# Float32 transposes that accumulate the tap sums of the first batch, and a shorter conversion of float64 weights

## The chip, the core and the metric

The kernel runs on one core of a Trainium2 chip. The metric is device time in microseconds (us) from launch to the last instruction; smaller is better. The engines are called TensorE (PE in the profile), VectorE (DVE), ScalarE (ACT), GpSimd (POOL) and SyncE (SP). Each runs its own instructions in program order and waits on semaphores for the others.

## What is computed

The reference is a windowed mix over time with softmax weights, then a two-stage mixer. Shapes: x is 8 x 4096 x 192 (batch, time, channel), the weights of the mix are 8 x 4096 x 8 heads x 7 taps, the four mixer matrices arrive as float64.

```python
w = softmax(weight_gen, axis=-1)                       # 7 taps per head
out[b,s,h,g] = sum_k w[b,s,h,k] * x_pad[b, s+k, h, g]  # 6 zeros in front of each batch
xt = out.transpose(0, 2, 1)
h  = relu(xt @ w_tok1) @ w_tok2                        # mixes over time, 4096 -> 256 -> 4096
u  = out + h.transpose(0, 2, 1)
h2 = relu(u @ w_ch1) @ w_ch2                           # mixes over channels, 192 -> 1536 -> 192
result = u + h2
```

## The kernel before, in words

A batch is cut into 8 chunks of 512 time steps (CT = 4 steps in each of 128 partitions); with 8 batches there are 64 chunks. The program has two parts.

**The first batch** (lines 876 to 962) has no mixer work to run beside. For each chunk m it does the following.

- VectorE multiplies x by the softmax weights for all 7 taps, in two instructions (`products`, line 327, tiles called prk: four taps, then three). The seventh product is added to the fifth by an accumulating DMA that GpSimd issues (line 330).
- TensorE adds the remaining six products into PSUM by multiplying each with an identity matrix (`sums`, line 341, tile tapsum, 12 matmuls of 384 columns per chunk; the trace shows a float32 matmul as two passes). ScalarE copies the sum to SBUF (line 346, tile xa: the attention output of the chunk).
- Between the first four taps and the other two, TensorE does work of the chunk before: the first token matmul, 8 instructions (`token1_first`, line 517, tile th), and the turn of xa to channel-major form by 8 matmuls against the identity (`turn_first`, line 353, tile turn). ScalarE copies the turned chunk out (line 360) into xb (chunks 0 and 1) or into ts, which ScalarE's DMA queue spills to DRAM (lines 363 and 364). Chunks 6 and 7 are not turned here: in the main part VectorE turns them (line 291) and SP stores them (line 297).
- Meanwhile float64 weights are converted to float32 with integer steps on their two 32-bit halves (`convert`, lines 144 to 160). ScalarE makes a mask in three steps (lines 154 to 156), VectorE combines shifted bits in three (lines 158 to 160). One conversion of 1024 columns per chunk turns out the token weights w1 of that chunk; conversions of 768 columns for the channel weights are put between (w1 halves for chunks 1 and 3, c2 for chunk 5 and after), and the token weights w2 follow. raw tiles hold the float64 input; three of them take turns, so a load waits until VectorE has finished the conversion three loads before.
- The softmax of the next two chunks (lines 178 to 187) runs in odd chunks; its exponential (line 180) is on ScalarE, between a subtraction (179) and a sum (181) on VectorE.

The order of instructions here is the order of the code, with `run` taking turns between lists of steps.

At the end of the batch come the last token matmul, h1 = relu of the result in two parts (lines 474 and 476), and `token2(0)` (line 534), which also needs the first converted and split w2 weights (cast on ScalarE and difference on VectorE, lines 165 and 166).

**The main part** (from line 963) goes over the 64 chunks. For each: twelve column blocks of `channel1` (line 599, tiles ph) in six pairs, relu in two parts by ScalarE and VectorE (605, 606, tile h), `channel2` (line 617, into acc), the turn of the result (671, 672) and its store. `token1` and `token2` of later chunks, the attention of the next batch (`attention`, lines 210, 224 and 228) and the remaining conversions are put between them by a planner, `pump`, which works with estimated costs and times. ScalarE and VectorE split the weights of the last channel matrix on lines 459 to 461 (tile w2s).

Of the kernel before, what the change touches and what calls it, by code (L numbers as in the profile page):

```python
# [12 lines left out]
F32 = mybir.dt.float32  # L13
F32R = mybir.dt.float32r
U32 = mybir.dt.uint32
AF = mybir.ActivationFunctionType
# [5 lines left out]
def mixer_kernel(ctx: ExitStack, tc: tile.TileContext, x, wg, wt1, wt2, wc1, wc2, out):  # L22
    nc = tc.nc
# [20 lines left out]
    SM = 2  # L44
    XA = 4
    PR = 5
    FT = NCH - 2
    TAPS = [(0,), (1, 2), (3, 4), (5, 6)]
    Q = 32

# [4 lines left out]
    ctx.enter_context(tc.manual_schedule())  # L55
    pro = None

    below = const.tile([P, 1], F32, name="below")
    nc.gpsimd.memset(below, -float(np.nextafter(np.float32(2.0 ** -15), np.float32(0))))

# [50 lines left out]


    NV = 1024
    LOW30 = float(np.array(0x3FFFFFFF, np.uint32).view(np.float32))

    staged = {"raw": 0, "val": 0}
    raw_tag, tag_of = {}, {}
# [1 line left out]
    def raw_tile(tag=None):  # L121

        n = staged["raw"]
        staged["raw"] += 1
        if pro is not None and n % 3 == 0:
            return pro.tile([P, NV, 2], U32, tag="raw", name="raw")
        if tag is None:
            tag = "w1" if (n - n // 3 - 1) % 2 else "raw"
        raw_tag[n] = tag
        return p1.tile([P, NV, 2], U32, tag=tag, name="raw")  # L130

    def val_tile():

# [10 lines left out]
    def convert(raw, n, out):  # L144

        yield "gate", 0, lambda: state["vals"] < 2
        state["vals"] += 1
        yield "w", 0, lambda: free["val"]
        v = val_tile()[:, 0:n]
        out.append(v)  # L150
        bits = v.bitcast(U32)
        low, high = raw[:, 0:n, 0], raw[:, 0:n, 1]
        act, stt = nc.scalar.activation, nc.vector.scalar_tensor_tensor
# [4 lines left out]
        yield "v", cost, lambda: stt(bits, high, 3, bits, op0=ALU.logical_shift_left, op1=ALU.bitwise_and)  # L158
        yield "v", cost, lambda: stt(bits, low, 29, bits, op0=ALU.logical_shift_right, op1=ALU.bitwise_or)
        yield "v", cost, lambda: stt(bits, high, 0xC0000000, bits, op0=ALU.bitwise_and, op1=ALU.bitwise_or)  # L160

    def split(hi, lo, v):

# [157 lines left out]
    def products(m, pro):  # L321
        src, (wn, j) = xt.pop(m), wnt.pop(m)
        prs = []
        for k0, k1 in ((0, KA), (KA, K)):
            pr = pro.tile([P, KA, CT, D], F32, tag="pr", name="prk", bufs=3)[:, 0:k1 - k0]
            x_k, w = taps(src, wn, j, k0, k1)
            nc.vector.tensor_mul(pr.rearrange("p k t (h g) -> p k (t h) g", h=H), x_k, w)
# [6 lines left out]
    def sums(m, prs, between):  # L334
        acc = new_xa(m)
        ps = ps_pro.tile([P, 2, 512], F32, tag="sum", name="tapsum", bufs=2)
        half = CT // 2
        for k0, k1 in ((0, KA), (KA, len(prs))):
            for n in range(2):
                for k in range(k0, k1):  # L340
                    nc.tensor.matmul(ps[:, n, 0:half * D], ident, prs[k][:, n * half:(n + 1) * half, :],  # L341
                                     start=k == 0, stop=k == len(prs) - 1)
            if k0 == 0:
                between()
        for n in range(2):
            nc.scalar.copy(acc[:, n * half:(n + 1) * half, :], ps[:, n, 0:half * D])

    def turn_first(m):

        ps = ps_pro.tile([P, 2, 512], F32, tag="turn", name="turn")  # L350
        for n, d in enumerate((0, D - P)):
            for c in range(CT):
                nc.tensor.matmul(ps[:, n, c * P:(c + 1) * P], xat[m][:, c, d:d + P], ident, start=True, stop=True)  # L353
# [4 lines left out]
        for n, c0 in ((0, 0), (1, DC)):  # L358
            to = t[c0:P, n, :].rearrange("p (n b c) -> p c n b" if m == 0 else "p (n c b) -> p c n b", c=CT, b=Q)
            nc.scalar.copy(to, ps[c0:P, n, :].rearrange("p (c n b) -> p c n b", c=CT, b=Q))  # L360
# [469 lines left out]
    def prefetch(m):  # L830

        if m % SM == 0:
            load_wg(m)
        load_x(m)
# [41 lines left out]
    with tc.tile_pool(name="pro", bufs=1) as pro, \  # L876
            tc.tile_pool(name="ps_pro", bufs=1, space=bass.MemoryType.PSUM) as ps_pro:
        ident = pro.tile([P, P], F32, name="ident")
        make_identity(nc, ident)
        warm = pro.tile([P, 1], F32, name="warm")  # L880
        nc.scalar.activation(warm, ident[:, 0:1], AF.Exp)
        prefetch(0)
        th = ps_pro.tile([P, 2, 512], F32, tag="th", name="th")

        def token1_first(m, v):
            token1_float(th, v.rearrange("p (c r) -> p c r", c=CT), m,
                         0 if m == 0 else None, CT - 1 if m == NCH - 1 else None)

        def start(items):

            items = iter(items)
            for _ in range(5):
                next(items)[2]()
            return items

        between = {1: ("w1", 0), 3: ("w1", 1), 5: ("c2", 0)}
        w1_v, w1_it = {}, {}

        def start_w1(m):
            fetch_w1(m)  # L900
            w1_v[m] = []
            w1_it[m] = start(convert(rawt.pop(("w1", m)), CT * R, w1_v[m]))

        def others():

            if m > 0:
                token1_first(m - 1, v_old)
                turn_first(m - 1)

        run(softmax(0))  # L910
        start_w1(0)
        prefetch(1)
        start_w1(1)
        behind, channel = (), None
        for m in range(NCH):
            prs = products(m, pro)
            if m + AHEAD < NCH:
                prefetch(m + AHEAD)
            run(w1_it.pop(m), softmax(m + 1) if (m + 1) % SM == 0 and m + 1 < NCH else ())
            v, = w1_v.pop(m)  # L920
            if m == NCH - 1:
                fetch_channel("w1", 2)
                run(w2_it, until="n")
                fetch_w2(1)
                run(w2_it)
                token1_first(m - 1, v_old)
                sums(m, prs, lambda: None)
            if m == NCH - 2:
                load_wg(NCH)
            current, channel = channel, None  # L930
            if m in between:
                fetch_channel(*between[m])
                channel = start(convert_channel(*between[m], pro))
            if m + 2 < NCH:
                start_w1(m + 2)
            elif m + 2 == NCH:
                fetch_w2(0)
            nc.sync.dma_start(s0[m], v)
            run(behind)
            behind = ()  # L940
            if m == NCH - 2:
                sums(m, prs, others)
# [4 lines left out]
            if m < NCH - 2:  # L947
                sums(m, prs, others)
# [12 lines left out]
        pro = None  # L961
        state["vals"] = 1
# [198 lines left out]
```

## Time and profile before

| | us |
|---|---|
| median of 3 runs | 2110.72 (2109.53 to 2110.96) |
| profiled execution, first to last instruction | 2109.3 |
| TensorE busy | 2071.5 (98%) |
| VectorE busy | 1539.7 (73%) |
| ScalarE busy | 1444.6 (68%) |
| GpSimd busy | 165.1 (8%) |
| first matmul of token2(0), the end of the first batch | 118.30 |

The trace holds no time before the first and after the last instruction; the span of 2109.3 lies 1.4 us under the median of the runs. Busy shares are averages over the whole program, and the two parts have different limits. So the profile is read here by stretches: busy time per engine in a window, and timelines, where each row has the start, the length, the engine and line, what it writes and reads, how many instructions are merged, and in brackets how long the engine was idle before it and what released it.

### The profile page before, as it was taken

How to read it: one execution, taken by the hardware profiler on the slowest of the kernel's cores; microseconds unless marked ns; L12 is line 12 of the kernel's file. 1: busy time of each engine (PE TensorE's matmuls, PEld its weight loads, DVE VectorE, ACT ScalarE, POOL GpSimd, SP SyncE). 2: the span in 40 equal slices, each digit the busy share in tenths (PEclk: the TensorE clock that was granted, in tenths of full speed). 3: DMA queues.
4: the chain of work that ended last, by engine and by line, in shares of the span. 5: the costliest groups of instructions: out<-in, count | busy, mean ns of one | idle time of the engine just before them, and what ended most of it. 6: DMA issues, size and time to landing. Idle time of an engine off the chain costs nothing.

```text
span 2109.3 us, 32111 instructions
## 1 busy us (share of the span) xinstructions
PE 2071.5 (98%) x12736; PEld 1684.9 (80%) x12736; DVE 1539.7 (73%) x1760; ACT 1444.6 (68%) x2226; POOL 165.1 (8%) x202
## 2 busy tenths in 40 slices
PE   6989999999999999999999999999999999999998
PEld 4767888788887888888888888888888888888887
DVE  8979988888888777777777787777777765343433
ACT  5578776677776676667667667666766766676665
POOL 1001111000101000000000010000100000000000
PEclk9999999999999999999999999999999999999999
DMA  9965767777876776666666676666666555321221
GB/s 298 270 222 170 202 179 226 239 199 210 239 217 179 205 202 170 189 158 180 173 198 175 191 185 163 174 184 199 177 184 192 149 169 138 90 71 51 57 63 23
DMA packets 167350, 366.97 MB, mean 174 GB/s; under 512 B 16680, under 2 KB 106024, under 8 KB 151840
## 3 DMA queue, kind: packets, MB, share of 16 engines
q1 hardware_dynamic: 139808, 285.74, 42.6%
q0 software_dynamic: 26496, 77.61, 18.9%
q8 instruction: 100, 1.64, 0.3%
q10 hardware_dynamic: 896, 1.57, 0.2%
q14 instruction: 50, 0.41, 0.1%
HBM read 225.13 MB, written 70.52 MB: 140 GB/s over the span
## 4 chain that ended last, share of the span: by engine, by line
PE 93%; DVE 4%; DMA 1%; ACT 1%; issue 0%; SPq 0%; POOL 0%; ACTq 0%; DVEq 0%; POOLq 0%
PE acc L617 40%; PE ph L599 35%; PE up L534 7%; PE th L497 4%; PE tapsum L341 3%; PE th L517 2%; PE th L499 2%; DVE h L606 1%; DVE pr L210 1%; PE turn L353 1%; PE acc L634 0%; DMA xt<-in_x_dram 0%; DMA prk<-prk 0%; DMA out_dram<-out_tile 0%; DVE pr L224 0%
## 5 line engine op out<-in xcount | busy, mean ns | idle before, releaser
L617 PE MATMUL acc<-h,w2s 128*128 128x512 f32 x3800 | 886.8, 391 | 4.1 <-DVE w2s L460 4.1
L617 PEld LDWEIGHTS acc<-h,w2s 128*128 128x128 f32 x3800 | 710.8, 188 | 151.0 <-DVE w2s L460 4.5
L605 ACT ACTIVATE h<-ph 128x1024 fp32r<-128x1024 f32 x384 | 394.5, 1027 | 345.6 <-PE ph L599 298.1
L606 DVE SCALAR_TENSOR_TENSOR h<-ph,h 128x1024 fp32r<-128x1024 f32 x384 | 468.2, 1220 | 117.4 <-ACT h L605 116.6
L599 PE MATMUL ph<-u_hi,w_hi 64*128 64x512 f32 x2304 | 337.9, 394 | 5.3 <-DVE h L606 3.7
L599 PE MATMUL ph<-u_lo,w_hi 64*128 64x512 f32 x2304 | 329.3, 388 | 0.5 <-ACT u_lo L574 0.3
L599 PE MATMUL ph<-u_hi,w_lo 64*128 64x512 f32 x2304 | 328.1, 387 | 0.0
L210 DVE TENSOR_TENSOR pr<-xt,wg 128x768 f32<-128x768 f32 x336 | 311.3, 947 | 0.3
L599 PEld LDWEIGHTS ph<-u_hi,w_hi 64*128 64x128 f32 x2304 | 213.7, 184 | 72.5 <-issue 19.4
L599 PEld LDWEIGHTS ph<-u_lo,w_hi 64*128 64x128 f32 x2304 | 219.0, 184 | 47.3 <-ACT u_lo L574 0.7
L599 PEld LDWEIGHTS ph<-u_hi,w_lo 64*128 64x128 f32 x2304 | 218.4, 184 | 46.7
L228 POOL DMA_DIRECT2D xa<-pr x168 | 144.7, 861 | 1392.4 <-DVE pr L224 846.9
L681 ACT COPY out_tile<-oa 32x256 f32<-32x256 f32 x504 | 203.5, 404 | 8.0
L546 DVE TENSOR_TENSOR uf<-up,uf 64x512 f32<-64x512 f32 x63 | 43.0, 683 | 213.6 <-ACT uf L542 213.6
L534 PE MATMUL up<-w,h 128*128 128x512 f32 x630 | 161.0, 401 | 2.1 <-ACT up L528 2.1
L224 DVE TENSOR_TENSOR pr<-pr 128x768 f32<-128x768 f32 x168 | 160.1, 953 | 3.4
L534 PEld LDWEIGHTS up<-w,h 128*128 128x128 f32 x630 | 114.2, 188 | 43.4 <-issue 13.4
L528 ACT COPY up<-xb 128x1024 f32<-128x1024 f32 x63 | 64.1, 1017 | 75.5 <-DVE h L606 70.2
L269 DVE TENSOR_TENSOR xh<-xa,xh 128x768 fp32r<-128x768 f32 x48 | 45.8, 954 | 91.4 <-ACT xh L266 91.3
L497 PE MATMUL th<-xh,w 128*128 128x384 f32 x384 | 112.5, 358 | 0.0
L681 ACT COPY out_tile<-oc 32x256 f32<-32x256 f32 x252 | 101.6, 403 | 6.9 <-DVE oc L674 2.4
L499 PE MATMUL th<-xh,w 128*128 128x192 f32 x384 | 96.2, 250 | 0.0
(89 smaller groups left out, 1709.3 us busy)
## 6 DMA issues: line engine op xcount, KB each, us to landing
w<-s SPq DMA_DIRECT2D x96, 1024.0 KB, 5.5
xa<-pr POOLq DMA_DIRECT2D x168, 384.0 KB, 5.1
xt<-in_x_dram SPq DMA_DIRECT2D x56, 960.0 KB, 7.6
out_dram<-out_tile SPq DMA_DIRECT2D x128, 192.0 KB, 4.0
xs<-t SPq DMA_DIRECT2D x58, 384.0 KB, 4.6
xb<-xs SPq DMA_DIRECT2D x348, 64.0 KB, 5.2
raw<-in_moe_w_tok_dram SPq DMA_DIRECT2D x16, 1024.0 KB, 6.0
s<-w POOLq DMA_DIRECT2D x8, 1024.0 KB, 7.0
```

Source lines behind the costliest of these rows:

```text
L210: nc.vector.tensor_mul(t.rearrange("p t (h g) -> p (t h) g", h=H).rearrange("p (o n) g -> p o n g", o=1), x_k, w)
L224: nc.vector.tensor_add(sums[m], sums[m], prt.pop(m))
L228: nc.gpsimd.dma_start(xat[m].rearrange("p t d -> p (t d)"), sums[m].rearrange("p t d -> p (t d)"), accum_op=ALU.add)
L497: nc.tensor.matmul(th[:, r, 0:2 * D], w[:, c, 0, rs], xh[:, c, :], start=i + c == 0, stop=False, skip_group_check=True)
L499: nc.tensor.matmul(th[:, r, 0:D], w[:, c, 1, rs], xh[:, c, 0:D], start=False, stop=c == CT - 1, skip_group_check=True)
L528: nc.scalar.copy(up.rearrange("p k (n b c) -> p (k n) c b", c=CT, b=Q), xb.rearrange("p k (n c b) -> p (k n) c b", c=CT, b=Q))
L534: nc.tensor.matmul(up[:, n, :], h1[:, k, d], w[:, l, k * N:(k + 1) * N], start=k == 0 and j == 0 and not seeded, stop=k == KR - 1 and j == ...
L599: nc.tensor.matmul(ph[:, j, :], w[rows, k, p * P:(p + 1) * P], u[rows, k], start=n == 0, stop=n == len(steps) - 1)
L605: nc.scalar.activation(h[:, :, 0, :], ph, AF.Relu)
L606: nc.vector.scalar_tensor_tensor(h[:, :, 1, :], ph, 0.0, h[:, :, 0, :].bitcast(F32), op0=ALU.max, op1=ALU.subtract)
L617: nc.tensor.matmul(acc[:, n, :], w2s[:, f, d], h[:, j, l, :], start=False, stop=f == NF - 1 and i == len(steps) - 1, skip_group_check=True)
L681: nc.scalar.copy(dst, src[to:to + Q].rearrange("p (n e d) -> p n e d", n=2, d=Q)[:, n])
```

## The change

Two things are changed, both in the first batch and in every conversion.

1. *Tap sums.* All seven products are summed on TensorE, by transposes in transpose mode: the product is the stationary operand, the identity the moving one, and PSUM accumulates the seven results (42 transposes of 128 x 128 per chunk). The DMA that added the seventh product is gone. The sum comes out turned, so the turn of `turn_first` is gone too: ScalarE copies the six 128-column blocks out once as they are (line 363, tile sum) and once as the turned chunk (line 375, five copies). Six further transposes (`turn_back`) turn the sum back to xa, in the middle of the next chunk's sums; `token1_first` of the chunk before follows after them. All eight chunks are turned and spilled here (FT = NCH), so VectorE's two turns in the main part are gone. The sums of a chunk are now issued ahead of the conversion steps of chunk m + 2 on ScalarE; the loads of these weights (`fetch_w1`) stay where they were.

2. *Conversion.* ScalarE makes two values: from the low half a number with the top three bits of it (tile few), and from the high half a float scaled by 2 to the power -112 (tile val). VectorE shifts val left by 3 and joins few (line 170), then joins the sign bit (line 171). That is two steps on each engine for three. The tile few takes a buffer that other tiles use at other times: half of a w2 tile or a pr tile in the first batch, the xh tile in the main part (one buffer).

The core of the diff:

```diff
-    FT = NCH - 2
+    FT = NCH
...
-        yield "s", 950, lambda: act(v, high.bitcast(F32), AF.Abs)
-        yield "s", 1050, lambda: act(v, v, AF.Sign, bias=below[:, 0:1])
-        yield "s", 950, lambda: act(v, v, AF.Relu, scale=LOW30)
+        yield "s", 950, lambda: act(few, low, AF.Copy, scale=THREE[0], bias=THREE[1])
+        yield "s", 950, lambda: act(v, high.bitcast(F32), AF.Copy, scale=2.0 ** -112)
         cost = 70 + n * 1.05
-        yield "v", cost, lambda: stt(bits, high, 3, bits, op0=ALU.logical_shift_left, op1=ALU.bitwise_and)
-        yield "v", cost, lambda: stt(bits, low, 29, bits, op0=ALU.logical_shift_right, op1=ALU.bitwise_or)
-        yield "v", cost, lambda: stt(bits, high, 0xC0000000, bits, op0=ALU.bitwise_and, op1=ALU.bitwise_or)
+        yield "v", cost, lambda: stt(bits, bits, 3, few, op0=ALU.logical_shift_left, op1=ALU.bitwise_or)
+        yield "v", cost, lambda: stt(bits, high, 0x80000000, bits, op0=ALU.bitwise_and, op1=ALU.bitwise_or)
...
-        last = prs.pop()
-        nc.gpsimd.dma_start(prs[KA].rearrange("p t d -> p (t d)"), last.rearrange("p t d -> p (t d)"),
-                            accum_op=ALU.add)
...
+    def transpose(out, data, start):
+
+        nc.tensor.matmul(out, data, ident, is_transpose=True, start=start, stop=True, skip_group_check=True)
+
+    NB = CT * D // P
+
+    def sums(m, prs, between=(), after=()):
+
+        ps = ps_pro.tile([P, 2, 512], F32, tag="sum", name="tapsum", bufs=2).rearrange("p k n -> p (k n)")
+        for k, pr in enumerate(prs):
+            if k == KA:
+                for do in between:
+                    do()
+            flat = pr.rearrange("p t d -> p (t d)")
+            for j in range(NB):
+                transpose(ps[:, j * P:(j + 1) * P], flat[:, j * P:(j + 1) * P], k == 0 and j % 4 == 0)
+        for do in after:
+            do()
+        sumt[m] = p1.tile([P, CT, D], F32, tag="pr", name="sum", bufs=PR).rearrange("p t d -> p (t d)")
+        nc.scalar.copy(sumt[m], ps[:, 0:NB * P])
...
+        for c in range(2):
+            for n, rows, j, of in ((0, slice(0, P), 0, slice(0, P)), (1, hi, 1, lo)) if c == 0 else \
+                    ((0, lo, 1, hi), (0, hi, 2, lo), (1, hi, 2, hi)):
+                nc.scalar.copy(to[n][rows, c], blocks[of, j])
...
+    def turn_back(m):
+
+        t = sumt.pop(m)
+        ps = ps_pro.tile([P, 2, 512], F32, tag="turn", name="turn").rearrange("p k n -> p (k n)")
+        for j in range(NB):
+            transpose(ps[:, j * P:(j + 1) * P], t[:, j * P:(j + 1) * P], j % 4 == 0)
+        nc.scalar.copy(new_xa(m).rearrange("p c d -> p (c d)"), ps[:, 0:NB * P])
...
             if m + 2 < NCH:
-                start_w1(m + 2)
+                fetch_w1(m + 2)
...
             run(behind)
             behind = ()
+            if m > 0:
+                sums(m, prs, (lambda: turn_back(m - 1),), (lambda: token1_first(m - 1, v_old),))
+            else:
+                sums(m, prs)
+            if m in between:
+                channel = start(convert_channel(*between[m], pro))
+            if m + 2 < NCH:
+                start_w1(m + 2)
...
+        turn_back(NCH - 1)
         load_pair(NCH)
         token1_first(NCH - 1, v)
```

Three places show how the engines' orders move. The first is VectorE in an odd chunk of the first batch. Before, the three steps of the conversion are interleaved with the softmax of the next two chunks (mx and wg):

```order
L158 SCALAR_TENSOR_TENSOR val<-raw,val 128x1024
L178 TENSOR_REDUCE mx<-wg 128x64
L159 SCALAR_TENSOR_TENSOR val<-raw,val 128x1024
L179 TENSOR_TENSOR wg<-wg,mx 128x448
L160 SCALAR_TENSOR_TENSOR val<-raw,val 128x1024
L181 TENSOR_REDUCE mx<-wg 128x64
```

After, in the same place:

```order
L170 SCALAR_TENSOR_TENSOR val<-val,few 128x1024
L189 TENSOR_REDUCE mx<-wg 128x64
L171 SCALAR_TENSOR_TENSOR val<-raw,val 128x1024
L190 TENSOR_TENSOR wg<-wg,mx 128x448
L192 TENSOR_REDUCE mx<-wg 128x64
```

The sum (before line 181, now 192) follows the subtraction with no conversion step between them.

The second place is ScalarE at the end of the first batch, from the conversion of the first w2 weights to h1. Before:

```order
L154 ACTIVATE val<-raw 128x1024
L155 ACTIVATE val<-val,below 128x1024
L156 ACTIVATE val<-val 128x1024
L459 CAST w2s<-val 128x4x192
L154 ACTIVATE val<-raw 128x768
L155 ACTIVATE val<-val,below 128x768
L156 ACTIVATE val<-val 128x768
L165 CAST w_588<-val 128x1024
L346 COPY xa<-tapsum 128x384 x2
L474 ACTIVATE h_638<-th 128x2x192
```

After (ts_857 is the turned chunk 7, w_788 the first w2 weights):

```order
L482 CAST w2s<-val 128x4x192
L167 ACTIVATE few<-raw 128x768
L168 ACTIVATE val<-raw 128x768
L176 CAST w_788<-val 128x1024
L387 COPY xa<-turn 128x768
L363 COPY sum<-tapsum 128x768
L375 COPY ts_857<-tapsum 128x2x4x32
L375 COPY ts_857<-tapsum 64x2x4x32 x4
L378 DMA xs_863<-ts_857 128x512
```

Behind the cast of the w2 weights now stand the copies of chunks 6 and 7 (xa of chunk 6, the sum and the turned form of chunk 7, then xa of chunk 7), and h1 after them.

The third place is VectorE in the first chunk of the main part, around the last conversion of channel weights (128x768, whose result goes to w2s). Before:

```order
L166 TENSOR_TENSOR w_861<-val,w_861 128x1024
L291 STREAM_TRANSPOSE t<-xa 128x768
L606 SCALAR_TENSOR_TENSOR h<-ph,h 128x2x512
L181 TENSOR_REDUCE mx<-wg 128x64
L546 TENSOR_TENSOR uf<-up,uf 64x512
L158 SCALAR_TENSOR_TENSOR val<-raw,val 128x768
L159 SCALAR_TENSOR_TENSOR val<-raw,val 128x768
L160 SCALAR_TENSOR_TENSOR val<-raw,val 128x768
L460 TENSOR_TENSOR w2s<-val,w2s 128x4x64
```

After:

```order
L177 TENSOR_TENSOR w_1044<-val,w_1044 128x1024
L170 SCALAR_TENSOR_TENSOR val<-val,few 128x768
L171 SCALAR_TENSOR_TENSOR val<-raw,val 128x768
L629 SCALAR_TENSOR_TENSOR h<-ph,h 128x2x512 x2
L483 TENSOR_TENSOR w2s<-val,w2s 128x4x64
L484 TENSOR_TENSOR w2s<-val,w2s 128x4x128
L170 SCALAR_TENSOR_TENSOR val<-val,few 128x1024
L569 TENSOR_TENSOR uf<-up,uf 64x512
```

The conversion stands ahead of the update of u from token2 (uf, before line 546, now 569) and no longer behind it.

More of the change, by code (lines that the diff above doesn't have):

```diff
@@ L56, in mixer_kernel @@
     pro = None
-    below = const.tile([P, 1], F32, name="below")
-    nc.gpsimd.memset(below, -float(np.nextafter(np.float32(2.0 ** -15), np.float32(0))))
     w1_hi = const.tile([P, 3, F // 2], F32R, name="w1_hi")
@@ L115, in mixer_kernel @@
     NV = 1024
-    LOW30 = float(np.array(0x3FFFFFFF, np.uint32).view(np.float32))
     staged = {"raw": 0, "val": 0}
@@ L130, in raw_tile, with few_tile @@
         return p1.tile([P, NV, 2], U32, tag=tag, name="raw")
+    NEAR = 2.0 ** -10
+    THREE = 2.0 ** -29 * (1 - NEAR), -0.5 + 7.5 * NEAR
+    few = {}
+    def few_tile(n):
+        if pro is None:
+            return late.tile([P, CT, 2 * D], F32R, tag="xh", name="few").rearrange("p c d -> p (c d)")[:, 0:n].bitcast(U32)
+        if n <= CT * D:
+            return p1.tile([P, CT, D], F32, tag="pr", name="few", bufs=PR).rearrange("p c d -> p (c d)")[:, 0:n].bitcast(U32)
+        if not few:
+            few["both"], few["next"] = p1.tile([P, 2, NV], F32R, tag="w2", name="few"), 0
+        few["next"] ^= 1
+        return few["both"][:, few["next"], 0:n].bitcast(U32)
     def val_tile():
@@ L152, in convert @@
         low, high = raw[:, 0:n, 0], raw[:, 0:n, 1]
+        few = few_tile(n)
         act, stt = nc.scalar.activation, nc.vector.scalar_tensor_tensor
-        yield "s", 950, lambda: act(v, high.bitcast(F32), AF.Abs)
-        yield "s", 1050, lambda: act(v, v, AF.Sign, bias=below[:, 0:1])
-        yield "s", 950, lambda: act(v, v, AF.Relu, scale=LOW30)
+        yield "s", 950, lambda: act(few, low, AF.Copy, scale=THREE[0], bias=THREE[1])
+        yield "s", 950, lambda: act(v, high.bitcast(F32), AF.Copy, scale=2.0 ** -112)
         cost = 70 + n * 1.05
-        yield "v", cost, lambda: stt(bits, high, 3, bits, op0=ALU.logical_shift_left, op1=ALU.bitwise_and)
-        yield "v", cost, lambda: stt(bits, low, 29, bits, op0=ALU.logical_shift_right, op1=ALU.bitwise_or)
-        yield "v", cost, lambda: stt(bits, high, 0xC0000000, bits, op0=ALU.bitwise_and, op1=ALU.bitwise_or)
+        yield "v", cost, lambda: stt(bits, bits, 3, few, op0=ALU.logical_shift_left, op1=ALU.bitwise_or)
+        yield "v", cost, lambda: stt(bits, high, 0x80000000, bits, op0=ALU.bitwise_and, op1=ALU.bitwise_or)
     def split(hi, lo, v):
@@ L328, in products @@
             prs += [pr[:, k] for k in range(k1 - k0)]
-        last = prs.pop()
-        nc.gpsimd.dma_start(prs[KA].rearrange("p t d -> p (t d)"), last.rearrange("p t d -> p (t d)"),
-                            accum_op=ALU.add)
-        return prs
[L334 to L353, printed above, removed]
+        return prs
+    sumt = {}
+    def transpose(out, data, start):
[14 more added lines that the diff above has]
+        nc.scalar.copy(sumt[m], ps[:, 0:NB * P])
         if m < 2:
@@ L357, in turn_first @@
             t = pro.tile([P, 2, N], F32, tag="ts", name="ts0", bufs=2)
-        for n, c0 in ((0, 0), (1, DC)):
-            to = t[c0:P, n, :].rearrange("p (n b c) -> p c n b" if m == 0 else "p (n c b) -> p c n b", c=CT, b=Q)
-            nc.scalar.copy(to, ps[c0:P, n, :].rearrange("p (c n b) -> p c n b", c=CT, b=Q))
+        to = [t[:, n, :].rearrange("p (n b t c) -> p c t n b" if m == 0 else "p (n t c b) -> p c t n b", c=2, t=2, b=Q)
+              for n in range(2)]
+        blocks = ps[:, 0:NB * P].rearrange("p (t j n b) -> p j t n b", t=2, n=P // Q, b=Q)
+        lo, hi = slice(0, DC), slice(DC, P)
+        for c in range(2):
+            for n, rows, j, of in ((0, slice(0, P), 0, slice(0, P)), (1, hi, 1, lo)) if c == 0 else \
+                    ((0, lo, 1, hi), (0, hi, 2, lo), (1, hi, 2, hi)):
+                nc.scalar.copy(to[n][rows, c], blocks[of, j])
         if m >= 2:
@@ L891, in start @@
             items = iter(items)
-            for _ in range(5):
+            for _ in range(4):
                 next(items)[2]()
@@ L899, in start_w1 @@
         def start_w1(m):
-            fetch_w1(m)
             w1_v[m] = []
             w1_it[m] = start(convert(rawt.pop(("w1", m)), CT * R, w1_v[m]))
[L904 to L908, printed above, removed]
         run(softmax(0))
+        fetch_w1(0)
         start_w1(0)
         prefetch(1)
+        fetch_w1(1)
         start_w1(1)
@@ L925, in mixer_kernel @@
                 run(w2_it)
-                token1_first(m - 1, v_old)
-                sums(m, prs, lambda: None)
             if m == NCH - 2:
@@ L932, in mixer_kernel @@
                 fetch_channel(*between[m])
-                channel = start(convert_channel(*between[m], pro))
             if m + 2 < NCH:
-                start_w1(m + 2)
+                fetch_w1(m + 2)
             elif m + 2 == NCH:
@@ L940, in mixer_kernel @@
             behind = ()
+            if m > 0:
[6 more added lines that the diff above has]
+                start_w1(m + 2)
             if m == NCH - 2:
-                sums(m, prs, others)
                 w2_it = start(convert_w2(0))
@@ L946, in mixer_kernel @@
                 behind = current
-            if m < NCH - 2:
-                sums(m, prs, others)
             if m == NCH - 2:
```

## The prediction

> **What bounds the kernel now.** I read the windows first (busy time per stretch), then each engine's timeline in the first batch, then the waits. The columns of a window are its length, then busy us and count of TensorE, its weight loads, VectorE, ScalarE and GpSimd, the granted clock, the DMA share and GB/s.
>
> ```profile
> 0.00:118.30 118.30, 98.67 (x417) 69.83 (x417) 106.02 (x87) 63.20 (x80) 11.31 (x20) 0.97 0.91 278
> 118.30:160.00 41.70, 37.00 (x189) 29.34 (x190) 31.38 (x38) 31.11 (x40) 1.07 (x2) 0.88 0.63 224
> 160.00:200.00 40.00, 37.65 (x246) 29.37 (x247) 37.79 (x44) 35.73 (x51) 2.82 (x4) 1.00 0.56 178
> 900.00:1100.00 200.00, 200.00 (x1237) 164.76 (x1236) 145.95 (x173) 141.53 (x223) 16.24 (x19) 1.00 0.66 180
> ```
>
> Late in the program TensorE is busy 200.00 of 200 us and nothing of the change is there, so only the first 200 us can give or cost time. In the first batch (to 118.30) two engines are nearly full: VectorE with 106.02 of 118.30 us and TensorE with 98.67. The timelines tell which sets the pace. TensorE first (start, length, line, passes, and in brackets the idle time before with its cause):
>
> ```profile
> 12.67 6.97 PE L341 MATMUL tapsum<-prk,ident 128*128 128x384 f32 x16 [12.67 <-DVE prk L327]
> 24.14 10.62 PE L341 MATMUL tapsum<-prk,ident 128*128 128x384 f32 x24 [4.49 <-DMA prk<-prk]
> ...
> 49.32 1.95 PE L353 MATMUL turn<-ident,xa 128*128 128x128 f32 x16
> 51.10 7.91 PE L341 MATMUL tapsum<-prk,ident 128*128 128x384 f32 x24
> 58.85 2.76 PE L517 MATMUL th<-xa,val 128*128 128x192 f32 x16
> 61.45 1.95 PE L353 MATMUL turn<-ident,xa 128*128 128x128 f32 x16
> ...
> 114.10 2.87 PE L517 MATMUL th<-xa,val 128*128 128x192 f32 x16 [0.57 <-ACT xa L346]
> 118.30 2.56 PE L534 MATMUL acc<-w,h 128*128 128x512 f32 x10 [1.33 <-ACT w2s L459]
> ```
>
> By starts, a chunk costs TensorE 1.78 (turn) + 7.75 (sums) + 2.60 (th) = 12.13 us. Now VectorE:
>
> ```profile
> 9.26 5.83 DVE L327 TENSOR_TENSOR prk<-xt,wg 128x3072 f32<-128x3072 f32 x2 [1.72 <-DMA xt<-in_x_dram]
> ...
> 17.52 1.23 DVE L160 SCALAR_TENSOR_TENSOR val<-raw,val 128x1024 uint32<-128x1024 uint32 x1
> 18.66 5.82 DVE L327 TENSOR_TENSOR prk<-xt,wg 128x3072 f32<-128x3072 f32 x2
> ...
> 31.00 0.62 DVE L181 TENSOR_REDUCE mx<-wg 128x64 f32<-128x448 f32 x1 [2.05 <-ACT wg L180]
> ...
> 44.57 0.96 DVE L160 SCALAR_TENSOR_TENSOR val<-raw,val 128x768 uint32<-128x768 uint32 x1
> 45.44 5.82 DVE L327 TENSOR_TENSOR prk<-xt,wg 128x3072 f32<-128x3072 f32 x2
> ...
> 54.51 1.22 DVE L160 SCALAR_TENSOR_TENSOR val<-raw,val 128x1024 uint32<-128x1024 uint32 x1
> 55.65 0.61 DVE L181 TENSOR_REDUCE mx<-wg 128x64 f32<-128x448 f32 x1
> ...
> 81.44 0.62 DVE L181 TENSOR_REDUCE mx<-wg 128x64 f32<-128x448 f32 x1 [0.34 <-ACT wg L180]
> ...
> 102.33 1.22 DVE L158 SCALAR_TENSOR_TENSOR val<-raw,val 128x1024 uint32<-128x1024 uint32 x1
> 103.59 1.23 DVE L159 SCALAR_TENSOR_TENSOR val<-raw,val 128x1024 uint32<-128x1024 uint32 x1
> ```
>
> From 9.26 to 102.33, the end of the last chunk's products, VectorE idles only 2.05 and 0.34 us: 93.07 us for eight chunks, as slow as TensorE. A change has to lighten both.
>
> **The change part by part.** *Conversions.* The third VectorE step goes. By starts it is worth 18.66 - 17.52 = 1.14 us for 1024 columns and 45.44 - 44.57 = 0.87 for 768. The two steps that stay have the old shapes and keep the old price. Before 102.33 stand seven conversions of 1024 columns and three of 768: 7 x 1.14 + 3 x 0.87 = 10.6 us. The old idle of 2.4 goes too. Something comes back. ScalarE's exponential ran under the third step:
>
> ```profile
> 52.75 1.17 ACT L360 COPY xb<-turn 128x512 f32<-128x512 f32 x2
> ...
> 54.70 0.59 ACT L180 ACTIVATE wg<-wg 128x448 f32<-128x448 f32 x1
> ...
> 67.73 0.86 ACT L346 COPY xa<-tapsum 128x384 f32<-128x384 f32 x2 [0.66 <-ACT ts L360]
> ...
> 110.43 1.05 ACT L165 CAST w<-val 128x1024 fp32r<-128x1024 f32 x1 [0.43 <-DVE val L160]
> ```
>
> With that cover gone (the sum of line 181 follows the subtraction at once), VectorE waits 0.59 plus handover, 0.7, at three softmaxes: 2.1 us. The products would end 10.6 + 2.4 - 2.1 = 10.9 us sooner, at 91.4, **if nothing else is slower than 11 us a chunk**.
>
> *ScalarE's order.* Per chunk it loses a step of the conversion and gains one copy of 768 columns (0.86) and five turn copies of 256 (about 0.4 each by 1.17 for two of 512, so 2.0 for 1.17). It was busy 63.20 of 118.30 us, so the work is covered. The conversion of chunk m + 2 now stands behind the sum and turn copies of chunk m, which wait for TensorE; its load keeps its place in SP's queue. This load is issued when VectorE ends the conversion of chunk m:
>
> ```profile
> raw<-in_moe_w_tok_dram SPq DMA_DIRECT2D x16, 1024.0 KB, 6.0
> ```
>
> 6.0 us to land, two ScalarE steps of some 1.1, then 0.86 + 0.86 + 2.0 of copies: done after 12 us, while VectorE asks for the converted chunk 11 + 5.7 us on. Covered by 4 us; without that cover see rival 4. The new helper tile has one buffer in the main part: a second conversion's first ScalarE step waits for the first one's VectorE step, with h copies behind it. In the order that VectorE step stands well ahead, so I count nothing.
>
> *Tap sums.* Per chunk 24 passes of 322 ns (7.75/24) and 8 turns become 42 + 6 transposes of 128 columns. No transpose stands in this trace. Its nearest row is the turn of line 353: 8 matmuls in 1.78 us, 223 ns each, in two passes of 111. Upper bound 48 x 0.223 + 2.60 = 13.3 us a chunk; with one pass each, 48 x 0.111 + 2.60 = 7.9. I take 111 ns, because the compiled program holds one matmul instruction per transpose where a plain float32 matmul has two. Then TensorE waits for VectorE. The Trainium skill (TensorE: Matmul & The Clock Gate, section Terms) calls its transpose mode four times faster for float32; an estimate by it is 223/4 = 56 ns, 5.3 us a chunk. Either way VectorE sets the pace, and the sum is the same.
>
> *The accumulating DMA* goes; TensorE's 4.49 us wait at 24.14 goes with it, but VectorE never waited for it, so I count nothing. The DMA queues over the first batch (packets, MB, share of the time), and what SP's queue waited for (us in total, times, longest):
>
> ```profile
> q1 hardware_dynamic: 9303, 27.80, 71.6%
> q0 software_dynamic: 1183, 3.40, 14.7%
> q10 hardware_dynamic: 896, 1.57, 4.2%
> ```
>
> ```profile
> SPq L371 <- DVE val L160: 40.8, 5, 11.0
> ```
>
> Without q0, and with six chunks of spills in q10 for four, 71.6% + 6.3% of 118.3 us is 92 us of transfers; they fit into some 105. SP's raw loads wait 40.8 us for VectorE to free buffers, so they will come as much sooner.
>
> *The end of the batch.* Call P the end of the products. Before, token2(0) on line 534 starts at 118.30, P + 16.0. After, ScalarE's order puts the cast of token weights ahead of both turned-back copies: four VectorE steps of 1.26 (103.59 - 102.33) make P + 5.0, cast 1.05, copy 0.86 (6.9), th 2.87 (9.8), six transposes 0.7, copy 0.86 (11.4), th 2.87 (14.2), and h1 as before, 118.30 - 114.10 - 2.87 = 1.3, with handovers 15.9. TensorE idles 4 us there; after the 4.49 us at 24.14 the 24 passes took 10.62 for 7.91, so I add half of that, 1.4. The start moves to 91.4 + 17.3 = 108.7: **9.6 us sooner**.
>
> *The first chunk of the main part.*
>
> ```profile
> 138.48 7.12 PE L617 MATMUL acc<-h,w2s 128*128 128x512 f32 x30
> 145.44 2.43 PE L534 MATMUL up<-w,h 128*128 128x512 f32 x10
> ...
> 154.19 7.18 PE L617 MATMUL acc<-h,w2s 128*128 128x512 f32 x20 [4.05 <-DVE w2s L460]
> 161.29 0.97 PE L599 MATMUL ph<-u_hi,w_hi 64*128 64x512 f32 x6
> ...
> 169.95 0.96 PE L599 MATMUL ph<-u_hi,w_hi 64*128 64x512 f32 x6 [2.24 <-DVE h L606]
> ```
>
> TensorE waits 4.05 us for the last channel weights; then 20 matmuls take 7.10 where 20 cost 4.64 (6.96 for 30), so 2.5 more by the slow clock. The new order converts these weights ahead of the token2 copies, some 6 us sooner, so the wait should go. So should the 2.24: VectorE's conversion steps before that h are one where there were three. Together 8.8; I take 7.5, leaving 1.3 for waits that I do not see. Ends: 0, and 10 if the small waits go too. The two VectorE turns and later third steps lie beside a full TensorE: nothing.
>
> Sum: 9.6 + 7.5 = 17.1. The profiled execution has a span of 2109.3; the median of the runs is 2110.72, 1.4 above it. 2110.7 - 17.1 = **2093.6**.
>
> **Rivals.** (1) *Only the first batch gains*: the main part keeps its three losses because the earlier start brings its loads no sooner. SP's waits on VectorE speak against it. 2110.7 - 9.6 = 2101. (2) *Transposes cost as plain matmuls*, 13.3 us a chunk: TensorE runs from 12.67 for 8 x 13.3 = 106.2 us, plus some 3.2 of copies and h1: 122.1, later by 3.8; less 7.5 gives 2107. The single instruction speaks against it. (3) *Slower*: transposes do not release the clock. TensorE's clock read 0.97 in the first batch and 0.88 after it, where it stalled. At half of it a chunk costs 2 x 7.9 = 15.8 us: 12.67 + 126 + 4 = 143, later by 25; less 7.5, 2128. It decides from (118.3 + 7.5 - 12.7 - 3.2)/8 = 13.7 us a chunk. Against it: 2.60 us of plain matmuls stand in each chunk, and 7.9 us of work at full clock in 11. The Trainium skill, same page, Part 4, says that transposes do not count towards the full clock; nothing in this trace can show it. (4) *VectorE starves*: the 4 us of cover fail, ScalarE waits for a raw load and VectorE for ScalarE. Two us a chunk would return 14 of the 17 us: 2108.
>
> **How the numbers follow.** Forecast 0.64 (2086 to 2100), rival 1 0.15, rival 2 0.08, rival 3 0.05, rival 4 0.08. The low end takes all 8.8 and the small waits, no slow clock at the end, and 2 us more of the first batch: 2086. The high end, 2105, takes in rival 1. Within 0.2% (4.2 us, about what a measurement can tell from no change) lie parts of rivals 2 and 4: 0.06; slower 0.05; faster 0.89.
>
> **What would show it.** In the changed profile: products of the last chunk end near 91 us, line 557's first matmul starts near 109, each transpose takes 56 to 111 ns, VectorE idles about 0.7 us at three softmaxes and nowhere else before, and the wait of line 640 for the last w2s is gone. Transposes over 0.23 us, a first-batch clock near 0.5, or VectorE waiting on ScalarE for us per chunk would make it wrong.

## The result and the profile after

The changed kernel takes 2091.88 us (median of 4 runs, 2090.82 to 2095.53) where the kernel before, on the same chip, takes 2110.84 (4 runs, 2109.53 to 2113.31): a ratio of 0.9913, 95% interval 0.9899 to 0.9927, or 19.0 us less. The profiled execution took 2090.82 us with a span of 2089.0, so the two traces differ by 20.3 us.

The windows of the changed kernel come first, cut at the start of token2(0), now at 107.86. The columns are those of the prediction.

```profile
0.00:107.86 107.86, 73.98 (x512) 70.03 (x513) 91.32 (x74) 62.85 (x95) 4.36 (x11) 0.94 0.85 293
107.86:160.00 52.14, 51.38 (x318) 40.69 (x319) 44.77 (x53) 42.91 (x59) 2.49 (x4) 1.00 0.63 217
```

The first batch is 10.44 us shorter (118.30 to 107.86), and TensorE now has 34 us of idle time in it. Behind it TensorE is nearly full from the start: it idles 0.76 us in the second window, where it idled 4.70 of 41.70 before. From 900 to 1100 it is busy 200.00 of 200 us, as before.

VectorE's timeline in the first batch, the last column being the idle time ahead of a row and its cause:

```profile
8.46 5.83 DVE L338 TENSOR_TENSOR prk<-xt,wg 128x3072 f32<-128x3072 f32 x2 [0.54 <-DMA xt<-in_x_dram]
...
26.39 0.62 DVE L192 TENSOR_REDUCE mx<-wg 128x64 f32<-128x448 f32 x1 [0.64 <-ACT wg L191]
...
48.51 0.62 DVE L192 TENSOR_REDUCE mx<-wg 128x64 f32<-128x448 f32 x1 [0.78 <-ACT wg L191]
...
71.17 0.62 DVE L192 TENSOR_REDUCE mx<-wg 128x64 f32<-128x448 f32 x1 [0.64 <-ACT wg L191]
...
84.05 5.82 DVE L338 TENSOR_TENSOR prk<-xt,wg 128x3072 f32<-128x3072 f32 x2
89.79 1.22 DVE L170 SCALAR_TENSOR_TENSOR val<-val,few 128x1024 uint32<-128x1024 uint32 x1
```

The products run from 8.46 to 89.79: 81.33 us for eight chunks, 93.07 before. Between them VectorE idles only at the three sums of the softmax, 2.06 us in all. TensorE has become the waiting engine, as its timeline shows:

```profile
11.88 7.10 PE L346 MATMUL tapsum<-ident,prk 128*128 128x128 f32 x42 [11.88 <-DVE prk L338]
...
49.35 4.16 PE L540 MATMUL th<-xa,val 128*128 128x192 f32 x16 [1.91 <-ACT xa L387]
...
62.40 2.87 PE L540 MATMUL th<-xa,val 128*128 128x192 f32 x16 [2.14 <-ACT xa L387]
...
77.46 4.50 PE L346 MATMUL tapsum<-ident,prk 128*128 128x128 f32 x24 [2.58 <-DVE prk L338]
...
96.67 5.45 PE L540 MATMUL th<-xa,val 128*128 128x192 f32 x16 [3.76 <-ACT xa L387]
...
103.67 2.87 PE L540 MATMUL th<-xa,val 128*128 128x192 f32 x16 [0.89 <-ACT xa L387]
107.86 2.55 PE L557 MATMUL acc<-w,h 128*128 128x512 f32 x10 [1.33 <-ACT w2s L482]
...
126.88 7.12 PE L640 MATMUL acc<-h,w2s 128*128 128x512 f32 x30
...
136.10 6.96 PE L640 MATMUL acc<-h,w2s 128*128 128x512 f32 x30
142.99 0.97 PE L622 MATMUL ph<-u_hi,w_hi 64*128 64x512 f32 x6
```

Behind the first chunk TensorE waits for products in most chunks. The last rows answer to those of before: line 640 takes its last weights with no wait (the 4.05 us are gone), its second group of 30 takes 6.96 us, and the ph after it, at 161.29 before, starts at 142.99. That is 18.30 us sooner. Behind the second chunk's `channel2` it is 20.17 (the next ph starts at 172.47 for 192.64), with the 2.24 us wait for h gone too. At the next up it is 21.14 (185.10 for 206.24), where a wait of 0.62 us is gone as well. Near 654 us a wait for h of 2.51 us replaces one of 1.49, and the end is 20.3 us sooner.

### The profile page after: what moved, and what is told of

It is laid out like the page before. It is cut to its first block, busy times and chain, and to the rows that moved or that the text cites. A ratio compares the mean times of both kernels' runs of the same rounds, so it can differ in the third digit from the quotient of the medians.

```text
span 2089.0 us, 32247 instructions
## 1 busy us (share of the span) xinstructions
PE 2042.9 (98%) x12832; PEld 1682.9 (81%) x12832; DVE 1514.1 (72%) x1736; ACT 1434.4 (69%) x2232; POOL 159.5 (8%) x193
## 4 chain that ended last, share of the span: by engine, by line
PE 90%; DVE 6%; DMA 1%; ACT 1%; issue 1%; SPq 0%; POOL 0%; ACTq 0%; DVEq 0%; POOLq 0%
PE acc L640 40%; PE ph L622 36%; PE up L557 7%; PE th L520 4%; PE th L522 2%; DVE prk L338 2%; PE th L540 1%; DVE h L629 1%; DVE pr L221 1%; DVE val L170 1%; PE acc L657 0%; DMA out_dram<-out_tile 0%; DMA xt<-in_x_dram 0%; DVE val L171 0%; DMA raw<-in_moe_w_tok_dram 0%
## 6 DMA issues: line engine op xcount, KB each, us to landing
xt<-in_x_dram SPq DMA_DIRECT2D x56, 960.0 KB, 10.2
raw<-in_moe_w_tok_dram SPq DMA_DIRECT2D x16, 1024.0 KB, 10.2
```

## The experiments

Beside the conversion alone, the sums alone, transpose mode off and the late split the kernel before took 2110.69 us (14 runs); beside the other four it took 2111.39 (7 runs). Unless said otherwise each kernel is the changed one with one edit, and stages are read in the traces against it. P is the end of the products of the last chunk.

**The conversion alone**, in the kernel before:

```diff
-        yield "s", 950, lambda: act(v, high.bitcast(F32), AF.Abs)
...
+        yield "s", 950, lambda: act(few, low, AF.Copy, scale=THREE[0], bias=THREE[1])
...
-            for _ in range(5):
+            for _ in range(4):
```

> Theory (two engines were near full in the first batch, so each half of the change alone gains little there, and the gain of the main part belongs to the shorter conversion): token2(0) starts at 117 to 118.5 us (118.30 before, 107.86 with the whole change), because TensorE still needs 12.13 us a chunk from 24.1 us on; the main part gains 8 to 10 us; in all 2101 to 2103 us. Rival (the conversion is the whole change, TensorE only followed VectorE): token2(0) starts near 108 and the time is 2091 to 2093.

Measured: 2101.98 us (2101.65 to 2104.83), ratio 0.9963 (0.9950 to 0.9976). TensorE's timeline, then VectorE's:

```profile
88.31 7.91 PE L355 MATMUL tapsum<-prk,ident 128*128 128x384 f32 x24
...
100.43 2.75 PE L355 MATMUL tapsum<-prk,ident 128*128 128x384 f32 x8
...
119.12 2.53 PE L548 MATMUL acc<-w,h 128*128 128x512 f32 x10 [1.33 <-ACT w2s L473]
```

```profile
31.82 0.62 DVE L195 TENSOR_REDUCE mx<-wg 128x64 f32<-128x448 f32 x1 [4.49 <-ACT wg L194]
...
56.08 0.62 DVE L195 TENSOR_REDUCE mx<-wg 128x64 f32<-128x448 f32 x1 [2.44 <-ACT wg L194]
...
82.71 0.62 DVE L195 TENSOR_REDUCE mx<-wg 128x64 f32<-128x448 f32 x1 [4.60 <-ACT wg L194]
```

TensorE still needs 12.12 us a chunk (88.31 to 100.43), and VectorE gives the time it saves back in waits of 4.49, 2.44 and 4.60 us. The batch ends at 119.12, no sooner than before and 0.6 us above the forecast; its first product also starts 0.78 us later (10.04 for 9.26). So the whole gain lies in the main part, which takes 1982.9 us from token2(0) to the last instruction where it took 1991.0 (1981.1 in the changed kernel). Neither the 4.05 us nor the 2.24 us wait is left in it, although the order of the first batch is the old one. VectorE's timelines in the first chunk of the main part, before, here and in the changed kernel, show why:

```profile
149.12 0.68 DVE L546 TENSOR_TENSOR uf<-up,uf 64x512 f32<-64x512 f32 x1 [1.30 <-ACT uf L542]
149.87 0.96 DVE L158 SCALAR_TENSOR_TENSOR val<-raw,val 128x768 uint32<-128x768 uint32 x1
```

```profile
140.06 0.92 DVE L173 SCALAR_TENSOR_TENSOR val<-val,few 128x768 uint32<-128x768 uint32 x1
...
149.97 0.68 DVE L560 TENSOR_TENSOR uf<-up,uf 64x512 f32<-64x512 f32 x1 [0.83 <-ACT uf L556]
```

```profile
127.40 0.96 DVE L170 SCALAR_TENSOR_TENSOR val<-val,few 128x768 uint32<-128x768 uint32 x1 [0.37 <-ACT val L168]
```

With the short conversion the planner puts the last channel weights (128x768) ahead of the update of u (uf, in the changed kernel at 137.57), with the long one behind it. Counted from token2(0) their conversion starts 10.6 us sooner here, of which the two VectorE steps that are missing ahead of it explain about 2.

**The sums alone**: the changed kernel with the old conversion.

```diff
-        yield "s", 950, lambda: act(few, low, AF.Copy, scale=THREE[0], bias=THREE[1])
...
+        yield "s", 950, lambda: act(v, high.bitcast(F32), AF.Abs)
...
-            for _ in range(4):
+            for _ in range(5):
```

> Theory: VectorE still needs 93 us for the eight chunks, so the products end near 101.5 us, and with the longer end of the batch token2(0) starts at 118 to 122 us; the 4 us wait for the last w2s weights in the main part stays; in all 2108 to 2115 us. Rival (the tap sums are the whole change): token2(0) starts near 108 and the time is 2091 to 2100.

Measured: 2122.10 us (2118.18 to 2123.62), ratio 1.0051 (1.0036 to 1.0066): slower than before. TensorE's timeline:

```profile
119.76 2.51 PE L561 MATMUL acc<-w,h 128*128 128x512 f32 x10 [1.33 <-ACT w2s L486]
...
155.58 7.29 PE L644 MATMUL acc<-h,w2s 128*128 128x512 f32 x20 [4.05 <-DVE w2s L487]
...
172.59 0.97 PE L626 MATMUL ph<-u_hi,w_hi 64*128 64x512 f32 x6 [3.38 <-DVE h L633]
...
221.43 4.52 PE L544 MATMUL th<-xa,val 128*128 128x192 f32 x16 [3.29 <-DVE w L181]
```

The first batch ends at 119.76, inside the forecast of 118 to 122. The total missed: I had 2115 at most. In the main part the 4.05 us wait is there as before, a wait for h has grown from 2.24 to 3.38, and the token matmul at 221.43 waits 3.29 us for its weights and then runs at the slow pace (4.52 us for 2.87). The first batch (1.46), the longer wait (1.14) and this one (3.29 + 1.65) make 7.5 of the 10.7 us by which its span, 2120.0, is longer than that of before. Near 530 us there are new waits of 0.70 and 0.72, and near 687 a wait for h takes 2.45 for 1.49; the rest I have not traced. Why the planner places the conversion of those token weights so late here is not settled.

**Transpose mode off.** The same 48 operations per chunk as plain float32 matmuls, in the same order.

```diff
-        nc.tensor.matmul(out, data, ident, is_transpose=True, start=start, stop=True, skip_group_check=True)
+        nc.tensor.matmul(out, data, ident, start=start, stop=True, skip_group_check=True)
```

> Sums and turns by plain float32 matmuls against the identity in the place of transposes, all else as in the changed kernel. Theory (a transpose costs one pass of 109 ns, a plain matmul two; TensorE then needs 13.3 us a chunk and becomes the bound): token2(0) starts near 122 us, 2105 to 2107 us. Rival (transpose mode is not what helps; accumulating and turning in one go is): within 3 us of 2092.

Measured: 2107.84 us (2105.59 to 2110.80), ratio 0.9985 (0.9976 to 0.9995). TensorE's timeline:

```profile
90.70 5.52 PE L346 MATMUL tapsum<-ident,prk 128*128 128x128 f32 x48
96.05 1.50 PE L346 MATMUL turn<-ident,sum 128*128 128x128 f32 x12
...
104.02 5.52 PE L346 MATMUL tapsum<-ident,prk 128*128 128x128 f32 x48
...
123.93 2.32 PE L557 MATMUL acc<-w,h 128*128 128x512 f32 x9 [1.33 <-ACT w2s L482]
```

This is the second rival, made real. Each operation is two passes of 111 ns, a chunk costs 13.32 us (90.70 to 104.02) with no idle time, and token2(0) starts at 123.93, 1.9 us later than forecast; the time is 0.8 us above the range. Without the mode the kernel is 16 us slower than the changed one, and 5.9 slower than the conversion alone.

**The accumulating DMA put back**: GpSimd adds the seventh product to the fifth, so 36 transposes are left.

```diff
+        last = prs.pop()
+        nc.gpsimd.dma_start(prs[KA].rearrange("p t d -> p (t d)"), last.rearrange("p t d -> p (t d)"),
+                            accum_op=ALU.add)
         return prs
```

> The seventh product is added by the accumulating DMA again, the other six by transposes. Theory (the DMA cost nothing but a wait of TensorE that VectorE hides; TensorE has room): TensorE may wait 8 us for it in the first chunk, but the products end within 0.7 us of the changed kernel's and token2(0) starts within 3 us (the last chunk's sum waits for its DMA of some 5 us at the end). 2091 to 2095. Rival (the DMA took bandwidth and VectorE's time): products end 3 us later or more.

Measured: 2101.46 us (2098.88 to 2103.60), ratio 0.9949 (0.9932 to 0.9966), over 6 us above the top of the forecast. The waits of the first 120 us (total, times, longest), then VectorE's timeline, then TensorE's:

```profile
ACT sum L366 <- PE tapsum L349: 28.7, 7, 8.2
PE tapsum L349 <- DMA prk<-prk: 27.7, 7, 7.2
...
DVE mx L192 <- ACT wg L191: 11.1, 4, 7.6
```

```profile
33.46 0.62 DVE L192 TENSOR_REDUCE mx<-wg 128x64 f32<-128x448 f32 x1 [7.58 <-ACT wg L191]
...
93.22 5.82 DVE L338 TENSOR_TENSOR prk<-xt,wg 128x3072 f32<-128x3072 f32 x2
```

```profile
107.49 2.79 PE L349 MATMUL tapsum<-ident,prk 128*128 128x128 f32 x12 [6.16 <-DMA prk<-prk]
...
119.39 2.55 PE L560 MATMUL acc<-w,h 128*128 128x512 f32 x10 [1.33 <-ACT w2s L485]
```

VectorE never reads what the DMA makes, yet its products take 90.37 us (8.59 to 98.96), 9.04 more. The way there is through ScalarE. TensorE waits for the DMA; the sum's copy, now ahead of the conversion in ScalarE's order, waits for TensorE; and VectorE waits 7.58 us for the exponential behind both. The copy of chunk 0's sum waits 8.16 us and starts at 26.89, then the other copies and the conversion take until the exponential starts, at 32.87. In the kernel before, the exponential stood behind a sum's copy already, but with nothing between:

```profile
29.63 0.86 ACT L346 COPY xa<-tapsum 128x384 f32<-128x384 f32 x2 [3.47 <-PE tapsum L341]
30.38 0.59 ACT L180 ACTIVATE wg<-wg 128x448 f32<-128x448 f32 x1
```

This copy waits for the tap sums that waited 4.49 us for the DMA at 24.14, and VectorE's wait of 2.05 us at 31.00 is for this exponential. So the DMA reached VectorE before the change too, by the same way. After the last chunk the DMA delays the last 12 transposes, and token2(0) starts at P + 20.4 for 18.1.

**The third VectorE step put back**, in the first batch only (the last step done twice, with the same result).

```diff
+        if pro is not None:
+            yield "v", cost, lambda: stt(bits, high, 0x80000000, bits, op0=ALU.bitwise_and, op1=ALU.bitwise_or)
```

> The last VectorE step of each conversion is done twice in the first batch, and once in the main part; the result is the same. Theory (VectorE paces the first batch, the main part's gain belongs to the conversions there): seven steps of 1.14 and three of 0.87 less the 2.1 us in which they cover the exponential put the products' end 8.5 us later, token2(0) with two more steps starts near 118.5, the main part keeps its gain: 2102 to 2104 us. Rival (the main part's waits came from where the first batch ends): the main part gives back 4 us or more besides, 2107 or above.

Measured: 2103.90 us (2103.85 to 2104.25), ratio 0.9962 (0.9947 to 0.9977). VectorE's timeline, then TensorE's:

```profile
8.33 5.83 DVE L340 TENSOR_TENSOR prk<-xt,wg 128x3072 f32<-128x3072 f32 x2 [0.91 <-DMA xt<-in_x_dram]
...
93.10 5.82 DVE L340 TENSOR_TENSOR prk<-xt,wg 128x3072 f32<-128x3072 f32 x2
```

```profile
84.27 4.12 PE L348 MATMUL tapsum<-ident,prk 128*128 128x128 f32 x24 [2.97 <-DVE prk L340]
...
119.14 2.56 PE L559 MATMUL acc<-w,h 128*128 128x512 f32 x10 [1.33 <-ACT w2s L484]
```

The products take 90.51 us (8.33 to 98.84), 9.2 more; 8.5 were expected. With the fast sums TensorE waits for VectorE, so a step of VectorE is paid in full. The main part keeps 8.0 us of its gain of 9.9 (1983.0 us for 1991.0 before), and neither of its two waits is back; of the 1.8 us that it gives back, 1.16 are a slower first stretch, to which I come below.

**Two orders made better.** The first leaves the split of the first w2 weights (a cast on ScalarE, a difference on VectorE) until behind the sums of the last chunk; the second issues the softmax's instructions ahead of the conversion's, so that a conversion step again covers the exponential; the third kernel has both.

```diff
                 fetch_w2(1)
-                run(w2_it)
...
                 sums(m, prs)
+            if m == NCH - 1:
+                run(w2_it)
```

> Theory (at the end of the batch the cast of the w2 weights holds the copy of chunk 6 on ScalarE, and TensorE waits 3.76 us for it and then runs its 16 passes in 5.45 us for 2.87 at the slow clock): with the cast and its difference issued behind the sums, the first of the two waits goes, token2(0) starts at 101 to 103 us, and the time is 2086. Rival (the raw loads that land near 107 us bound the first chunk of the main part anyway): token2(0) sooner, but a new wait of 3 to 6 us behind it, 2090 to 2092.

```diff
-            run(w1_it.pop(m), softmax(m + 1) if (m + 1) % SM == 0 and m + 1 < NCH else ())
+            run(softmax(m + 1) if (m + 1) % SM == 0 and m + 1 < NCH else (), w1_it.pop(m))
```

> In odd chunks the softmax's steps take their turn ahead of the conversion's, so the second conversion step stands between the subtraction and the sum. Theory (VectorE sets the pace of the first batch and waited 0.64 to 0.78 us for the exponential at three softmaxes): these waits are gone, the products end 2 us sooner counted from their start, token2(0) starts 2 us sooner, 2089 to 2090 us. Rival (raw loads or ScalarE would hold VectorE anyway): the end does not move by more than 0.5 us.

> The late split and the covered exponential together. Theory: both gains add, token2(0) starts near 102.5 us, 2087 to 2088 us. Rival: the loads of the last weights bound the end, no better than 2089.7.

Measured: 2089.69 us (2087.50 to 2092.40), ratio 0.9901 (0.9886 to 0.9916), for the late split; 2089.61 (2088.78 to 2093.18), 0.9898 (0.9878 to 0.9917), for the hidden exponential; 2087.70 (2085.10 to 2089.63), 0.9884 (0.9868 to 0.9900), for both. TensorE's timeline with the late split:

```profile
95.37 2.87 PE L540 MATMUL th<-xa,val 128*128 128x192 f32 x16 [1.75 <-ACT xa L387]
...
104.49 2.53 PE L557 MATMUL acc<-w,h 128*128 128x512 f32 x10 [1.33 <-ACT w2s L482]
```

TensorE idles 1.75 us in place of 3.76 ahead of th, the 16 passes then take 2.87 us in place of 5.45, and token2(0) starts at P + 14.0 (P is 90.50) in place of P + 18.1. Hiding the exponential brings the products to 79.16 us, 2.17 less. Two forecasts missed: the late split was to take 2086 us with token2(0) at 101 to 103, and with both token2(0) was to start near 102.5. The intervals of these kernels overlap that of the changed kernel, so the times alone don't show a gain; the order is seen in the traces, where the kernel with both starts token2(0) at 103.84, 4.0 us sooner. The two gains do not add in full: TensorE still idles 2.49 us ahead of th, whose passes take 4.55. Near 650 us a wait for h takes 3.05 us in place of 2.51, and the span of that trace, 2086.6, is only 2.4 us shorter.

## Why the prediction was right, point by point

The forecast was 2093.6 us (2086 to 2105); 2091.88 was measured, and the mechanism was the one forecast. But one statement of the working was wrong, two terms were mis-sized, and some of the agreement is luck.

- *VectorE and TensorE together set the pace*: shown. The conversion alone leaves the first batch where it was, the sums alone make it 1.5 us longer, and the two together make it 10.4 shorter. The gains don't add: -8.7, +11.4 and, together, -19.0 us.
- *Products, 82.1 us for eight chunks* (9.26 to 91.4): 81.33. The mis-sized term is the removed step, at 1.14 and 0.87 us. These are the times by starts to an instruction that does not read its result; to a step that reads it, it is 1.26 (102.33 to 103.59), and 0.99 for 768 columns. In four of the seven conversions of 1024 columns, and in the three of 768, a step of this second kind goes, so the ten steps come to 11.4 us and not 10.6. Putting the third step back cost 9.2 us, where 8.5 were expected. Taking the exposed exponential away gave 2.17 (2.1 in the sum). The cover of 4 us for ScalarE's raw loads held: from the third chunk on ScalarE is done at least 5.6 us before VectorE asks (61.53 and 67.12), so the fourth rival did not come about.
- *A transpose takes one pass*: right. 24 take 2.67 us by starts, 111 ns each, and with plain matmuls the second rival's 2107 became 2107.84.
- *End of the batch, P + 17.3*: P + 18.07. The path is the one of the sum; the cast of the w2 weights stands ahead of the copies on ScalarE, and moving it away gave 4.1 us. The mis-sized term is the slow clock: 1.4 us forecast, 2.6 measured (5.45 for 2.87). It is not a fixed price: with the exponential hidden, a gap of 3.75 us cost 1.4 (4.25).
- *The accumulating DMA, "VectorE never waited for it"*: wrong. VectorE's wait of 2.05 us at 31.00 goes back to it by way of ScalarE, as shown above. The sum had these 2.05 us all the same, under the old idle time, so the forecast did not suffer. In the new order of ScalarE the DMA costs 9.6 us (2101.46 against 2091.88), where the forecast of that run had some 3 at most. What it cost in all within the old order was not tried.
- *The main part, 7.5 us*: 9.9, of which 8.8 are the three losses named, gone as forecast. The reason given, the new order, fits: counted from token2(0) the last channel weights are converted 12.0 us sooner (127.40 after 107.86, where it was 149.87 after 118.30; some 6 were forecast). What makes this order is the shorter conversion: with it alone the 4.05 us wait is gone, with the sums alone it is there. The shorter conversion without the new order was not tried. Behind 200 us the working saw nothing to win or lose; near 654 us 1.0 us is lost.
- *Luck*: the rest of the main part is the clock. One row is from the windows of before, the next from those of the changed kernel, the last from the kernel with the hidden exponential, all from token2(0) to the first channel2:

```profile
118.30:138.48 20.18, 19.54 (x124) 15.37 (x124) 14.87 (x18) 16.14 (x20) 0.53 (x1) 0.92 0.66 239
```

```profile
107.86:126.88 19.02, 18.36 (x124) 14.49 (x125) 16.27 (x19) 16.11 (x21) 0.53 (x1) 1.00 0.62 204
```

```profile
105.21:125.64 20.43, 19.34 (x124) 14.60 (x125) 16.46 (x19) 16.60 (x21) 0.53 (x1) 0.92 0.65 219
```

In the changed kernel the same 124 matmuls take 1.16 us less at a granted clock of 1.00 than at 0.92 before. But the kernel with the hidden exponential and the one with the third step, both with the changed sums, ran this stretch at 0.92, with TensorE busy 19.34 and 19.53 us, and the one with plain matmuls at 1.00, with 18.32. So nothing shows that this gain belongs to the change. Also, 0.8 us of the first batch's gain in these two traces is only that the first x landed sooner (products from 8.46, not 9.26); the start of the products lies between 8.2 and 10.0 in the ten traces. And the products (0.8 us less than forecast) and the end of the batch (0.8 more) cancel.

The third rival, slower because transposes don't release the clock, is refuted by the first 42 operations on TensorE, the transposes of the first chunk. In the windows of the changed kernel (length, TensorE's busy time and count, clock, DMA share, GB/s) the first two rows are these 42 (those that cross the border counted twice), the third 24 later ones, the fourth the slow th:

```profile
11.88:16.56 4.68, 4.68 (x22) 1.00 1.02 415
16.56:18.98 2.42, 2.42 (x22) 1.00 1.03 428
20.01:22.68 2.67, 2.67 (x24) 1.00 1.05 435
96.67:101.95 5.28, 5.28 (x16) 0.50 0.94 248
```

The first 22 take 213 ns each; the others take half of that, 2.42 us in all, like the 24 later ones (2.67/24 = 111 ns). No other matmul ran before 18.98, so the transposes by themselves brought the fast pace, within 4.7 us. (The clock column reads 1.00 in the slow stretch too, so at the start of a program it doesn't tell; the passes do.) The Trainium skill (TensorE: Matmul & The Clock Gate, Part 4) says that the full clock does not engage for transposes; the trace disagrees, with 213 ns at first and 111 later.

## What to carry to other kernels

When two engines are about equally full, a saving on one of them shows as a wait of the other: look for the pair of changes, and expect their gains not to add. When a step moves on an engine that works in order, ask again who waits behind it, for every producer of that step; a DMA that held VectorE up for 2.05 us when the sum's copy stood behind the conversion costs 9.6 us with the copy ahead of it. At the end of a stage, what the next stage needs should stand first in the order of the engine that serves both.

## What was not expected of the hardware

- A gap in TensorE's work can have a second price behind it, and the length of the gap alone does not decide it. In the changed kernel the 16 passes of th take 5.45 us behind a gap of 3.76, 4.16 behind one of 1.91, but 2.87 behind one of 2.14.
- A float32 transpose of 128 x 128 is repeated every 111 ns, half the 223 ns of a plain float32 matmul of that size (5.35 us for 24 without the mode, 90.70 to 96.05). The Trainium skill (TensorE: Matmul & The Clock Gate, Terms) has its transpose mode four times faster for float32; the trace has two times.
- The program's 16 loads of float64 token weights took a median of 10.2 us to land in place of 6.0, and cost VectorE nothing in the first batch:

```profile
raw<-in_moe_w_tok_dram SPq DMA_DIRECT2D x16, 1024.0 KB, 10.2
```
